# A light-weight convolution and a quick-GELU feed-forward: POOL sums and one tap's buffer change places

## The chip, the cores and the metric

One core of one Trainium2 chip runs the whole program. The metric is the time of one execution on the device in microseconds; less is better. Engines are named as in the profile: PE (TensorE: matmuls, PEld their weight loads), DVE (VectorE), ACT (ScalarE), POOL (GpSimd), SP (SyncE, which only issues DMAs). PSUM is the memory that PE writes; SBUF is the on-chip memory of all the others.

## What is computed

`x` has 8 batches of 4096 tokens of 192 channels. A causal convolution of 7 taps, whose weights are a softmax over the taps and are shared by 24 channels each, is followed by a feed-forward layer with 2048 hidden units. All is float32.

```python
def _attn_ref(x, weight):
    w = np.exp(weight - np.max(weight, axis=-1, keepdims=True))
    w = w / (np.sum(w, axis=-1, keepdims=True) + 1e-09)
    ...
    out = np.einsum('hk,bskhg->bshg', w, x_unf)      # x_unf: the last 7 tokens of each token
    return out.reshape(B, S, D)

def _moe_ref(x, w_in, w_out):                        # x: (32768, 192)
    h = x @ w_in
    g = h * (1.0 / (1.0 + np.exp(-1.702 * h)))
    return g @ w_out
```

## The kernel before

The 32768 tokens are worked on in 32 big steps. Each big step has two products. `hidden` (line 773) makes h and its GELU from the convolved x (the first product); `second` (line 1079) multiplies GELU(h) by w_out (the second product). Both use fast matrix multiplication: fewer matmuls than the plain product, in exchange for sums of operands before and of results after. Operands are summed in SBUF by DVE, by POOL and by accumulating DMAs; results are summed in PSUM and by DVE.

**The order is written by hand.** `HIDDEN` (line 738) and `PLAN` (line 1031) are lists of small actions; each engine gets its instructions in the order of these lists, and waits for others by semaphores. One execution of `hidden` runs `HIDDEN` once, one of `second` runs `PLAN` once. All of it is unrolled: `hidden(1), second(1), hidden(2), second(2), ...` An engine that waits holds back all that is queued behind on it.

- `("mm", v, t, to, first)` is one term of the first product: 4 matmuls of 512 columns into the PSUM tile `p<to>` (2 banks), there being 4 such tiles, p0 to p3. `HIDDEN` has 40 of them, and `("fetch",)` is a 41st: the first term of the next big step, left out in the last. The operand is a block of conv (`conv_t`, or for blocks 16 to 19 a place in `g`).
- `("copy", "a" or "v", dst, src, sign)` moves a PSUM tile by ACT or DVE, `join` adds two by DVE, `gelu` is ACT's GELU into `g`. The names k0 to k8 (`KS`, line 145) are SBUF tiles; k0 is `room[:, 1, :]`.
- `("main", form, spot, p, first)` and `("go", n)` in `PLAN` issue the second product's matmuls (line 1097); `side` adds a fourth chunk beside the three, whose result ACT copies out (line 1122). `sum` is a DVE sum of operands ("spots" of 128x1024 in SBUF), `acc` one by an accumulating DMA from POOL's queue (line 1073).

**Spots.** `spot(i)` (line 138) names a place of 128x1024 in SBUF: 0 and 1 lie in `osbs`, 2 to 4 in `room`, the others in `g`. `spot(2)` and k0 are the same memory. (s, 0) and (s, 2) below are the halves of spot s.

**The convolution** of big step n+2 is made during `second(n)` and the beginning of `hidden(n+1)`. `("tap",)` runs the next of 21 taps (line 559): ACT multiplies a shifted x by a tap's weight. They run over c = 1, 0, 2 (blocks of 64 channels; c = 1 is the middle one) and k = 0 to 6. Tap (c, 0) is written to the block itself, the others to a "home": the places listed in `TAP_SPOTS` and `TAP_HALVES` (lines 158 and 159), in order of k. For c = 2, POOL adds the homes one by one (line 565). For c = 1 and 0 a tree of accumulating DMAs from POOL's queue adds them (line 583): `LATER` (line 552) says behind which tap a stage (c, i, j) is issued, which adds home j to home i; i = 0 is the block itself. 17 of the taps run in `PLAN`, to tap (2, 2), and 4 in `HIDDEN`.

**The sums of conv** ("pieces"). Each term of the first product takes a block of conv or a sum of blocks. The raw blocks are 0 to 5 (c = 0: 0 and 1, c = 1: 2 and 3, c = 2: 4 and 5); blocks 6 to 15 are sums in one buffer in `conv_t`, so a block of the next big step may be written only when PE has read the old one for the last time. Blocks 16 to 19 lie in `g`, at spots 14 and 17 (`SPOT_V`). POOL makes them (`sum_of`, line 590; the instruction's line is 433 for a difference and 431 for a sum). Each block also has a crossed copy, its upper and lower 64 partitions exchanged, by two DMAs from SP's queue (`cross`, line 597). `over` in `HIDDEN` makes the two sums of block 12 and its crossing, `ve` blocks 13 and 14; the rest comes from `list_pieces` (line 649), which `("piece", n)` takes n at a time; `("late",)` runs all that is left ahead of the mark `None`, behind which the four sums of blocks 16 to 19 stand.

SP's queue also carries, in the order of the program, the output's stores (line 1025) and the loads of x (line 99).

Of the kernel before, what the change touches and what calls it, by code (L numbers as in the profile page):

```python
# [15 lines left out]
def kernel(  # L16
# [93 lines left out]
    sums = [psum.tile([P, TOK], F32, name=f"sums{h}") for h in range(2)]  # L110
# [5 lines left out]
    NG = 4  # L116
# [41 lines left out]
    TAP_SPOTS = {0: (10, 16, 15), 1: (1, 2, 11)}  # L158
    TAP_HALVES = {2: ((11, 2), (13, 0), (18, 0), (18, 2), (18, 0), (18, 2)), 3: ((12, 2), (16, 2), (15, 2), (16, 0), (15, 0), (12, 0))}
# [39 lines left out]
    def own(big):  # L199
        return conv_t[:, big % 2 * NR : big % 2 * NR + NR, :]  # L200

    SUMS_B = [
        (6, 1, "-", 5), (7, 2, "-", 4), (8, 12, "-", 2), (9, 2, "-", 3), (10, 0, "-", 12), (11, 14, "-", 8),
    ]
    SUMS_B_1 = [
# [4 lines left out]
    SUMS_E = [  # L210
        (13, 0, "-", 3), (14, 1, "-", 3),
    ]
    SUMS_S = [
        (15, 1, "-", 11),
    ]
    SUMS_L = [
        (16, 0, "-", 6), (17, 7, "-", 3), (18, 0, "-", 2), (19, 0, "-", 1),
# [321 lines left out]
    def conv(big, c, k, ns=slice(0, 2), times=vec.tensor_scalar_mul):  # L539
# [66 lines left out]
    def cross_spot(s):  # L606
        cross(spot(s)[:, 1:NG:2, :], spot(s)[:, 0:NG:2, :])
# [6 lines left out]
    LATE = sorted({s for s, k in SPOT_V.values()})  # L614

    def runs(b0, b1, n=3):
        return [(i, min(i + n, b1)) for i in range(b0, b1, n)]
# [16 lines left out]
    def make_late_1():  # L634
        for item in SUMS_L:
            sum_of(1, item, vec)
        for s in LATE:
            cross_spot(s)

    def make_rest_1():  # L640
        for item in SUMS_E + SUMS_S:
            sum_of(1, item, vec)
        for r in (V_S, V_E):
            if r[1] > r[0]:
                cross_run(1, *r, act.copy)
# [3 lines left out]
    def list_pieces(big):  # L649

        def add(f, *a):
            pieces.append(lambda: f(*a))

        for r in RAW_RUNS:
            add(cross_run, big, *r)
        if NV_E:
            add(cross_run, big, *V_E)
        for sums, block in ((SUMS_B, V_B), (SUMS_S, V_S)):
            for item in sums:
                add(sum_of, big, item)  # L660
            for r in runs(*block):
                add(cross_run, big, *r)
        pieces.append(None)
        for item in SUMS_L:
            add(sum_of, big, item)
        for s in LATE:
            add(cross_spot, s)
# [65 lines left out]
    def plain(u, m, n, v, slot, ks=range(NC), first=0):  # L733
# [39 lines left out]
    def hidden(big, tiles, work):  # L773
# [82 lines left out]
        def ve(i):  # L856
            if more:
                need(f"done {big + 1}")
                sum_of(big + 1, SUMS_E[i])

        do = dict(
            mm=mm, copy=copy, join=join, gelu=gelu, turn=turn, tap=tap, early=early, over=over, ve=ve,
# [154 lines left out]
    def store(big, n, o=None, queues=(nc.sync,) * 3):  # L1017
# [382 lines left out]
```

## Time and profile before

| | |
|---|---|
| runs of the kernel before | 2480.61 us median (2478.57, 2480.61, 2483.55) |
| the profiled execution, its own time | 2478.28 us |
| its span from the first to the last instruction | 2476.6 us |
| mean granted clock of TensorE | 0.968 |
| ACT busy, POOL busy | 1711.2 us (69%), 1093.7 us (44%) |
| DMA queues, share of 16 engines | POOL's (software) 44.7%, SP's (hardware) 27.2% |

A row such as `L710 PE MATMUL slot<-conv_t,w_in_s` reads: line 710 of the kernel, PE, a matmul into the tile `slot` from `conv_t` and `w_in_s`. Line 710 is the first product, line 1097 the second. In rows of waits, `A <- B: total, times, longest` says that A's engine sat idle and that B ended it. In a timeline, the columns are the start, the duration, then what ran, and in brackets the idle time before it and what ended that. In the table by windows, each row is a stretch of time: its length, then the busy time and (count) of PE, PEld, DVE, ACT and POOL, the granted clock of TensorE, the busy share of the DMA engines and GB/s.

### The profile page before, as it was taken

To read this page: it belongs to the slowest core of one execution; us is meant where nothing else is said; L and a number is where in the kernel's file an instruction comes from. 1 tells how busy PE (TensorE), PEld (TensorE's weight loads), DVE (VectorE), ACT (ScalarE), POOL (GpSimd) and SP (SyncE) were. 2 spreads that over 40 slices of the span, in tenths; PEclk is the share of its full clock that TensorE was granted. 3 is DMA by queue.
4 is the path that set the end of the run, shared out by engine and by line. 5 is a ranking of instruction groups with operands and counts; after the bars stand their busy time and mean duration, and the time that the engine had idled before them with its cause. 6 is when DMAs were issued, how large, how long until landed. Compare 5 with 4: busy or idle time off the path is not lost.

```text
span 2476.6 us, 63053 instructions
## 1 busy us (share of the span) xinstructions
PE 2336.8 (94%) x25090; PEld 1478.1 (60%) x25090; DVE 2129.1 (86%) x3059; ACT 1711.2 (69%) x3338; POOL 1093.7 (44%) x1218
## 2 busy tenths in 40 slices
PE   9899999999999999999999999999999999999999
PEld 4355656656665566556646565466666566764664
DVE  8998888898888988889888888888988888888898
ACT  8677676776666766767666677676776766767655
POOL 1553445434454444543445544455444554344520
PEclk9899999999999999999999999999999999999999
DMA  8976678866678666787667876678766788666753
GB/s 194 157 154 138 133 136 163 165 141 138 133 152 174 141 130 133 152 175 144 135 135 140 176 148 138 137 137 173 156 139 133 136 168 162 139 133 122 150 106 66
DMA packets 317127, 358.04 MB, mean 145 GB/s; under 512 B 123680, under 2 KB 226592, under 8 KB 316832
## 3 DMA queue, kind: packets, MB, share of 16 engines
q0 software_dynamic: 82192, 196.32, 44.7%
q1 hardware_dynamic: 232992, 157.29, 27.2%
q8 instruction: 199, 3.26, 0.5%
q14 instruction: 96, 0.79, 0.1%
q10 hardware_dynamic: 1648, 0.39, 0.1%
HBM read 53.15 MB, written 25.17 MB: 32 GB/s over the span
## 4 chain that ended last, share of the span: by engine, by line
PE 73%; DMA 13%; DVE 5%; issue 4%; POOL 3%; ACT 1%; SPq 0%; POOLq 0%; ACTq 0%; DVEq 0%
PE slot L710 34%; PE slot L1097 16%; PE sums L710 12%; PE sums L1097 11%; DMA g<-g 7%; DMA conv_t<-room 3%; DMA osbs<-osbs 3%; POOL g L433 1%; ACT room L800 1%; POOL conv_t L583 1%; POOL g L583 1%; DVE g L433 1%; DVE room L433 0%; DMA g<-in_moe_w_in_dram 0%; POOL g L1073 0%
## 5 line engine op out<-in xcount | busy, mean ns | idle before, releaser
L710 PE MATMUL slot<-conv_t,w_in_s 64*128 64x512 f32 x3372 | 935.4, 613 | 8.0 <-DVE osbs L1014 6.5
L1097 PE MATMUL slot<-g,w_form 128*32 128x256 f32 x5872 | 716.1, 379 | 6.5 <-DMA g<-g 5.7
L710 PEld LDWEIGHTS slot<-conv_t,w_in_s 64*128 64x128 f32 x3372 | 552.8, 196 | 252.0 <-issue 132.3
L433 DVE TENSOR_TENSOR g<-g 128x1024 f32<-128x1024 f32 x372 | 444.9, 1221 | 31.5 <-ACT g L826 28.2
L433 POOL TENSOR_TENSOR conv_t<-conv_t 128x256 f32<-128x256 f32 x300 | 283.8, 1018 | 399.5 <-PE slot L710 202.3
L1097 PE MATMUL sums<-g,w_form 128*32 128x256 f32 x3800 | 425.5, 379 | 6.8 <-DMA g<-g 6.6
L1097 PEld LDWEIGHTS slot<-g,w_form 128*32 128x32 f32 x5872 | 361.3, 110 | 100.9 <-DMA g<-g 12.0
L710 PE MATMUL sums<-conv_t,w_in_s 64*128 64x512 f32 x1284 | 408.4, 603 | 0.3 <-DVE w_in_s L416 0.3
L819 ACT ACTIVATE g<-slot 128x512 f32<-128x512 f32 x494 | 265.8, 624 | 129.4 <-PE slot L710 94.7
L565 POOL TENSOR_TENSOR conv_t<-conv_t,g 128x512 f32<-128x512 f32 x180 | 267.8, 1488 | 145.2 <-ACT g L563 140.3
L1097 PE MATMUL slot<-g,w_out_s 128*32 128x256 f32 x4080 | 321.3, 379 | 0.0
L1122 ACT COPY room<-slot 32x256 f32<-32x256 f32 x434 | 158.9, 366 | 220.9 <-PE slot L1097 214.4
L563 ACT ACTIVATE g<-xt,cw 128x512 f32<-128x512 f32 x418 | 287.7, 717 | 3.7
L710 PEld LDWEIGHTS sums<-conv_t,w_in_s 64*128 64x128 f32 x1284 | 209.0, 192 | 91.9 <-issue 43.5
L1097 PEld LDWEIGHTS sums<-g,w_form 128*32 128x32 f32 x3800 | 208.1, 110 | 80.8 <-DMA g<-g 13.5
L710 PE MATMUL slot<-g,w_in_s 64*128 64x512 f32 x556 | 201.0, 642 | 56.0 <-ACT room L800 48.1
L1097 PEld LDWEIGHTS slot<-g,w_out_s 128*32 128x32 f32 x4080 | 166.2, 110 | 125.8 <-ACT g L819 11.4
L1073 POOL DMA_DIRECT2D g<-g x124 | 126.9, 1023 | 231.6 <-DVE g L433 156.4
L800 ACT COPY room<-slot 128x512 f32<-128x512 f32 x246 | 137.4, 627 | 109.0 <-PE slot L710 48.8
L826 ACT ACTIVATE g<-g 128x1024 f32<-128x1024 f32 x155 | 170.4, 1100 | 0.4 <-DVE g L813 0.4
L1122 ACT COPY room<-sums 32x256 f32<-32x256 f32 x217 | 79.5, 366 | 115.5 <-PE sums L1097 110.6
L583 POOL DMA_DIRECT2D g<-g x145 | 147.3, 1016 | 26.1 <-ACT g L563 24.3
(246 smaller groups left out, 3973.5 us busy)
## 6 DMA issues: line engine op xcount, KB each, us to landing
g<-g POOLq DMA_DIRECT2D x124, 512.0 KB, 7.2
conv_t<-conv_t SPq DMA_DIRECT2D x240, 192.0 KB, 3.2
xin<-in_x_dram SPq DMA_DIRECT2D x240, 180.0 KB, 6.4
g<-g POOLq DMA_DIRECT2D x149, 256.0 KB, 6.6
out_dram<-osbs SPq DMA_DIRECT2D x186, 128.0 KB, 4.0
g<-g SPq DMA_DIRECT2D x124, 128.0 KB, 4.0
g<-room POOLq DMA_DIRECT2D x31, 512.0 KB, 6.6
conv_t<-g POOLq DMA_DIRECT2D x60, 256.0 KB, 4.7
```

Of the source, the lines that this page charges most:

```text
L433: eng.tensor_sub(v(dst), v(a), v(b))
L563: act.mul(home, conv_src(big, c, k), cw[:, c, k : k + 1])
L565: nc.gpsimd.tensor_add(dst, dst, home)
L583: nc.gpsimd.dma_start(out=out, in_=src, accum_op=ALU.add)
L710: nc.tensor.matmul(slot[h], w_in_s[halves[h], a, v * P : (v + 1) * P], src, start=first, stop=True, skip_group_check=True,)
L800: act.copy(out, i) if sign > 0 else act.mul(out, i, -1.0)
L819: act.activation(dst[:, :, h, :], ot(bank(src, h)), AF.Gelu_apprx_sigmoid, scale=float(sign))
L826: act.activation(dst.rearrange("p o h t -> p h o t"), src, AF.Gelu_apprx_sigmoid, scale=float(sign))
L1073: nc.gpsimd.dma_start(out=spot(dst), in_=spot(a), accum_op=ALU.add)
L1097: nc.tensor.matmul(dst, w, t, start=first, stop=last, skip_group_check=True)
L1122: act.copy(to, d)
```

## The change

Per big step the same 15 POOL sums are made, in another place. Blocks 8, 6 and 7 go from `PLAN` to `HIDDEN`, where blocks 13 and 14 already were; these five now stand at five places (`ve` 0 to 4). Block 15 stays in `PLAN`. Of the four sums at spots 14 and 17, block 19 goes from the end of `PLAN` to the following `HIDDEN` (`vl`), for the same big step. Each of these four is crossed behind its own sum, by two DMAs of 64x256, where two DMAs of 64x2x256 crossed a whole spot. The homes of the middle block (c = 1) for k = 1 to 6 were (1,0), (1,2), (2,0), (2,2), (11,0), (11,2); they become (1,0), (1,2), (11,0), (2,0), (2,2), (11,2). Five stages of the tap trees are issued behind later taps, and the pieces stand elsewhere in `PLAN`. The order of the instructions on PE, DVE and ACT is as before, but for the place that ACT's taps 3 to 5 of the middle block write.

```diff
-    TAP_SPOTS = {0: (10, 16, 15), 1: (1, 2, 11)}
+    TAP_SPOTS = {0: (10, 16, 15)}
...
+    TAP_HALVES = {1: ((1, 0), (1, 2), (11, 0), (2, 0), (2, 2), (11, 2)), 2: ...
...
-    SUMS_B = [
-        (6, 1, "-", 5), (7, 2, "-", 4), (8, 12, "-", 2), (9, 2, "-", 3), (10, 0, "-", 12), (11, 14, "-", 8),
-    ]
+    SUMS_H = [
+        (13, 0, "-", 3), (8, 12, "-", 2), (14, 1, "-", 3), (6, 1, "-", 5), (7, 2, "-", 4),
+    ]
+    SUMS_M = [
+        (9, 2, "-", 3), (10, 0, "-", 12), (11, 14, "-", 8), (15, 1, "-", 11),
+    ]
+    RUNS_H, RUNS_M = [(6, 9), (13, 15)], [(9, 12), (15, 16)]
...
-        (16, 0, "-", 6), (17, 7, "-", 3), (18, 0, "-", 2), (19, 0, "-", 1),
+        (16, 0, "-", 6), (17, 7, "-", 3), (18, 0, "-", 2),
+    ]
+    SUMS_LH = [
+        (19, 0, "-", 1),
     ]
...
     LATER = {
-        (1, 2): [(1, 1, 2)], (1, 4): [(1, 3, 4)], (1, 6): [(1, 5, 6), (1, 0, 1)], (0, 3): [(1, 3, 5)],
-        (0, 2): [(0, 1, 2)], (0, 4): [(0, 3, 4)], (0, 6): [(0, 5, 6), (0, 0, 1)], (2, 0): [(1, 0, 3)],
-        (2, 2): [(0, 3, 5)], (2, 5): [(0, 0, 3)],
+        (1, 2): [(1, 1, 2)], (1, 4): [(1, 3, 4)], (1, 6): [(1, 5, 6)], (0, 0): [(1, 0, 1)], (0, 2): [(0, 1, 2)],
+        (0, 4): [(0, 3, 4)], (0, 5): [(1, 3, 5)], (0, 6): [(0, 5, 6)], (2, 0): [(0, 0, 1)], (2, 2): [(1, 0, 3)],
+        (2, 3): [(0, 3, 5)], (2, 5): [(0, 0, 3)],
     }
...
-    def cross_spot(s):
-        cross(spot(s)[:, 1:NG:2, :], spot(s)[:, 0:NG:2, :])
+    def cross_spot(b):
+        both = pair(0, b)
+        cross(both[:, 1, :], both[:, 0, :])
...
         for r in RAW_RUNS:
             add(cross_run, big, *r)
-        if NV_E:
-            add(cross_run, big, *V_E)
-        for sums, block in ((SUMS_B, V_B), (SUMS_S, V_S)):
-            for item in sums:
-                add(sum_of, big, item)
-            for r in runs(*block):
-                add(cross_run, big, *r)
+        for r in RUNS_H:
+            add(cross_run, big, *r)
+        for item in SUMS_M:
+            add(sum_of, big, item)
+        for r in RUNS_M:
+            add(cross_run, big, *r)
         pieces.append(None)
         for item in SUMS_L:
             add(sum_of, big, item)
-        for s in LATE:
-            add(cross_spot, s)
+            add(cross_spot, item[0])
...
         def ve(i):
             if more:
                 need(f"done {big + 1}")
-                sum_of(big + 1, SUMS_E[i])
+                sum_of(big + 1, SUMS_H[i])
+
+        def vl(i):
+            if big > 1:
+                sum_of(big, SUMS_LH[i])
+                cross_spot(SUMS_LH[i][0])
```

`HIDDEN`, one action to a line, where it differs:

```diff
 ('mm', 0, 19, 3, 0)
 ('join', 'p1', 'p2', '+', 'k7')
+('vl', 0)
...
 ('over',)
+('ve', 0)
 ('mm', 0, 5, 1, 0)
...
 ('mm', 1, 17, 3, 0)
+('ve', 1)
...
 ('mm', 1, 1, 3, 1)
-('ve', 0)
-('ve', 1)
+('ve', 2)
...
 ('join', 'p1', 'k1', '-', 'k7')
+('ve', 3)
 ('copy', 'a', 'k4', 'p3', 1)
 ('mm', 1, 15, 2, 0)
+('ve', 4)
```

`PLAN` differs in its `piece` and `late` actions alone. Before, the pieces ahead of `late` (13: seven sums and six crossings) stood one by one, the first two together, behind the `go`s 2 to 27 of its 78, `late` behind the 30th, and the last six as 1, 1, 1, 1 and 2 behind the `go`s 60, 62, 64, 66 and 67. Now ten (four sums and six crossings) stand behind the `go`s 2 to 26, `late` behind the 27th, and the last six, three sums each with its crossing, as 2, 2 and 2 behind the `go`s 60, 62 and 64.

More of the change, by code (lines that the diff above doesn't have):

```diff
@@ L157 @@
     KEPT_LATE = 3
-    TAP_SPOTS = {0: (10, 16, 15), 1: (1, 2, 11)}
-    TAP_HALVES = {2: ((11, 2), (13, 0), (18, 0), (18, 2), (18, 0), (18, 2)), 3: ((12, 2), (16, 2), (15, 2), (16, 0), (15, 0), (12, 0))}
+    TAP_SPOTS = {0: (10, 16, 15)}
+    TAP_HALVES = {1: ((1, 0), (1, 2), (11, 0), (2, 0), (2, 2), (11, 2)), 2: ((11, 2), (13, 0), (18, 0), (18, 2), (18, 0), (18, 2)), 3: ((12, 2), (16, 2), (15, 2), (16, 0), (15, 0), (12, 0))}
     def kept(i):
@@ L209 @@
     SUMS_F = [(12, 1, "+", 4), (12, 12, "-", 5)]
-    SUMS_E = [
-        (13, 0, "-", 3), (14, 1, "-", 3),
-    ]
-    SUMS_S = [
-        (15, 1, "-", 11),
+    SUMS_ES = [
+        (13, 0, "-", 3), (14, 1, "-", 3), (15, 1, "-", 11),
     ]
     SUMS_L = [
-        (16, 0, "-", 6), (17, 7, "-", 3), (18, 0, "-", 2), (19, 0, "-", 1),
+        (16, 0, "-", 6), (17, 7, "-", 3), (18, 0, "-", 2),
+    ]
+    SUMS_LH = [
+        (19, 0, "-", 1),
     ]
@@ L613 @@
     FIRST = V_F if NV_F else (FB, FB + 1)
-    LATE = sorted({s for s, k in SPOT_V.values()})
     def runs(b0, b1, n=3):
@@ L634, in make_late_1 @@
     def make_late_1():
-        for item in SUMS_L:
+        for item in SUMS_L + SUMS_LH:
             sum_of(1, item, vec)
-        for s in LATE:
-            cross_spot(s)
+        for b in SPOT_V:
+            cross_spot(b)
     def make_rest_1():
-        for item in SUMS_E + SUMS_S:
+        for item in SUMS_ES:
             sum_of(1, item, vec)
@@ L665, in list_pieces @@
             add(sum_of, big, item)
-        for s in LATE:
-            add(cross_spot, s)
+            add(cross_spot, item[0])
     def next_piece(n=1):
@@ L744 @@
         ("mm", 0, 18, 0, 0), ("tap",), ("mm", 0, 17, 2, 1), ("join", "k8", "p1", "-", "k2"),
[19 rows of a table removed]
[17 rows of a table added]
+        ("early", 5), ("gelu", 14, "p1", 1), ("mm", 1, 18, 0, 0), ("gelu", 12, "p2", 1), ("early", 2),
+        ("gelu", 15, "p0", 1), ("gelu", 13, "o13", 1),
     ]
@@ L858, in ve @@
                 need(f"done {big + 1}")
-                sum_of(big + 1, SUMS_E[i])
+                sum_of(big + 1, SUMS_H[i])
[3 more added lines that the diff above has]
+                cross_spot(SUMS_LH[i][0])
         do = dict(
-            mm=mm, copy=copy, join=join, gelu=gelu, turn=turn, tap=tap, early=early, over=over, ve=ve,
+            mm=mm, copy=copy, join=join, gelu=gelu, turn=turn, tap=tap, early=early, over=over, ve=ve, vl=vl,
             fetch=lambda: fetch(big + 1, tiles[NEXT[0]]) if more else None,
@@ L1031 @@
     PLAN = [
[36 rows of a table removed]
[7 rows of a table added]
+        ("sum", 0, 0, "+", 5), ("main", 14, 2, "p2", 0), ("go", 2), ("acc", 15, 4), ("piece", 1), ("tap",),
[7 rows of a table added]
+        ("sum", 13, 18, "+", 4), ("tap",), ("go", 2), ("sum", 6, 9, "-", 5), ("tap",), ("go", 1), ("acc", 12, 9),
[19 rows of a table added]
     ]
```

105 rows, old and new, of tables (HIDDEN, PLAN) are left out of this document.

## The prediction

> **What bounds the kernel now.** I read the page's engine rows first, then PE's waits.
>
> ```profile
> span 2476.6 us, 63053 instructions
> ...
> PE 2336.8 (94%) x25090; PEld 1478.1 (60%) x25090; DVE 2129.1 (86%) x3059; ACT 1711.2 (69%) x3338; POOL 1093.7 (44%) x1218
> ```
>
> ```profile
> PE sums L710 <- ACT room L800: 54.8, 15, 4.3
> PE slot L710 <- ACT room L800: 48.1, 13, 4.6
> ...
> PE sums L1097 <- DMA g<-g: 6.6, 11, 1.3
> PE slot L1097 <- DMA g<-g: 5.7, 8, 1.4
> ```
>
> PE is the engine with the least idle time, and nearly all of it has one releaser: 28 waits of 102.9 us together, 3.7 us each, for an ACT copy into `room`. They come once per big step, at the beginning of the first product. The waits of the second product sum to 12.3 us. What one wait costs in all is seen when the first products, `hidden(2)` to `hidden(30)`, are cut out as 29 windows, the second products behind them as 29 more, and the last big step beside them.
>
> ```profile
> 1177.40:1220.40 43.00, 39.25 (x168) 30.90 (x164) 35.33 (x50) 29.19 (x54) 18.31 (x21) 0.92 0.53 107
> 1254.90:1296.40 41.50, 37.86 (x168) 18.20 (x164) 33.12 (x50) 29.30 (x54) 18.06 (x20) 0.96 0.55 111
> ...
> sum 1223.10, PE 1113.82 PEld 773.58 DVE 1002.05 ACT 847.36 POOL 526.06; mean PE 38.41 PEld 26.68 DVE 34.55 ACT 29.22 POOL 18.14
> ```
>
> ```profile
> 1910.30:1944.60 34.30, 33.98 (x625) 20.07 (x624) 30.97 (x43) 24.12 (x51) 17.41 (x22) 1.00 1.00 196
> ...
> sum 999.10, PE 986.22 PEld 582.28 DVE 900.39 ACT 689.34 POOL 493.80; mean PE 34.01 PEld 20.08 DVE 31.05 ACT 23.77 POOL 17.03
> ```
>
> ```profile
> 2402.10:2437.30 35.20, 35.20 (x168) 16.74 (x164) 30.17 (x47) 26.67 (x50) 0.87 (x1) 1.00 0.19 38
> 2437.30:2471.20 33.90, 33.85 (x625) 20.15 (x624) 29.67 (x43) 12.94 (x34) 4.28 (x5) 1.00 0.45 85
> ```
>
> ```profile
> 1206.41 0.86 PE sums L710 x4
> ```
>
> The mean first product is 1223.10 / 29 = 42.18 us. The last one, with no taps around it and no wait, takes 35.20 us for 40 terms; with the 41st (4 matmuls, 0.86 us by the chain's row) 36.06. So each of the 29 loses 6.12 us, 177 us in all: 3.7 us as the wait and some 2.4 us since the clock granted behind it is halved for a while (0.92 or 0.96 over the window, 1.00 in the last). The second product has 34.45 us against 33.90, 16 us in all. These 193 us are all there is to win.
>
> Who is late at that place? The chain of waits over one boundary, PE's, ACT's and POOL's timelines there:
>
> ```profile
> 1254.22 0.68 POOL g L433
> 1254.90 5.67 DMA conv_t<-room
> ```
>
> ```profile
> 1254.87 1.13 PE L710 MATMUL slot<-conv_t,w_in_s 64*128 64x512 f32 x4
> ...
> 1261.36 1.66 PE L710 MATMUL slot<-g,w_in_s 64*128 64x512 f32 x3 [3.64 <-ACT room L800]
> ```
>
> ```profile
> 1255.42 1.34 ACT L563 ACTIVATE g<-xt,cw 128x512 f32<-128x512 f32 x2
> 1260.67 1.07 ACT L800 COPY room<-slot 128x512 f32<-128x512 f32 x2 [3.91 <-DMA conv_t<-room]
> ```
>
> ```profile
> 1247.09 0.86 POOL L583 DMA_DIRECT2D room<-g  x1 [3.18 <-DVE sums L431]
> ...
> 1251.70 0.73 POOL L433 TENSOR_TENSOR g<-conv_t 128x256 f32<-128x256 f32 x1 [2.85 <-DVE osbs L1014]
> ...
> 1253.53 2.05 POOL L433 TENSOR_TENSOR g<-conv_t 128x256 f32<-128x256 f32 x2
> 1254.90 1.50 POOL L583 DMA_DIRECT2D conv_t<-room  x1
> ```
>
> `conv_t<-room` is stage (1, 0, 3), behind tap (2, 0): the middle block takes up the home of its third tap, (2,0), which is `room[:, 1, :]`, which is k0. The ACT copy is k0 from p1, the first evacuation of the first product. It may not overwrite k0 before that stage has read it, at 1260.57, and the term of block 16, the fourth, needs p1. On POOL the stage stands behind the sums of blocks 16 to 18.
>
> **The change, part by part.**
>
> *The third tap's place, and the stages.* Spot 2 now holds taps 4 and 5. Its readers are the stages (1, 3, 4), early, and (1, 3, 5), behind tap (0, 5); stage (1, 0, 3) reads spot 11, which `hidden` writes only in its middle (GELUs 5 and 7). Stage (1, 3, 5) is today's `room<-g`, at 1247.09; behind tap (0, 5) and one more DMA of the kind (0.86 us) it would be issued at about 1248.
>
> ```profile
> room<-g POOLq DMA_DIRECT2D x29, 256.0 KB, 6.4
> ...
> conv_t<-conv_t SPq DMA_DIRECT2D x122, 64.0 KB, 3.1
> ```
>
> ```profile
> g<-g SPq DMA_DIRECT2D x124, 128.0 KB, 4.0
> ```
>
> With 6.4 us it lands at 1254.4, before PE begins the first product and more than 2 us before ACT could write k0. The wait goes: gain 6.12 us a step. Five stages spread over later taps add no DMA; (0, 0, 3) still stands behind tap (2, 5), and the sums behind it have till the 41st term. I cost them at nothing; were block 12 late, the wait would stand at that term, 31 us in.
>
> *A new wait.* The third tap now writes spot 11, which DVE reads in `sum 20, 20, -, 11`, the last of three, and PE in the two `go`s just before the tap.
>
> ```profile
> 1232.32 3.61 DVE L433 TENSOR_TENSOR g<-g 128x1024 f32<-128x1024 f32 x3
> ```
>
> ```profile
> 1235.19 0.72 ACT L563 ACTIVATE room<-xt,cw 128x512 f32<-128x512 f32 x1
> ```
>
> The tap ran at 1235.19, the DVE sums end at 1235.93: ACT is 0.74 us later. Queued behind on ACT are the seed of p1 for a term six `go`s on and the copies of PE's side chunks; six `go`s are 2.6 us (33.90 / 78 each), so PE need not wait. I cost it at nothing, 0.74 a step if that cover were gone.
>
> *What is late next* decides what is left of the 6.12 us.
>
> (a) ACT's two taps end at 1256.76, 1.89 us after PE's start at 1254.87; copying k0 takes 1.07, so p1's halves are free at about 2.4 and 3.0. PE wants them behind three terms, at 2.57: 0 to 0.5 us, I take 0.3.
>
> (b) The fifth term needs p0, which DVE empties into k5 behind the last joins and transposes of the second product.
>
> ```profile
> 1177.45 1.13 PE L710 MATMUL sums<-conv_t,w_in_s 64*128 64x512 f32 x4
> ```
>
> ```profile
> 1178.39 2.95 DVE L431 TENSOR_TENSOR room<-room 96x256 f32<-96x256 f32 x1
> ...
> 1181.74 1.25 DVE L802 COPY g<-slot 128x512 f32<-128x512 f32 x2
> ...
> 2403.07 0.38 DVE L431 TENSOR_TENSOR room<-room 96x256 f32<-96x256 f32 x1
> ```
>
> ```profile
> 1179.18 3.28 POOL L565 TENSOR_TENSOR conv_t<-conv_t,g 128x512 f32<-128x512 f32 x2
> ```
>
> That join of 0.38 us takes 2.95 beside POOL's adds, and the copy ends at 1182.99, 5.54 us after PE's start; without the delay of 2.57 it would be 2.97. PE wants the tile behind four terms, at 3.43. So 0 to 2.1 us. One POOL sum (block 19) no longer stands ahead of the adds, so the join should find its gap sooner, after the first add: I take 0.5.
>
> (c) The crossed half of block 16. Before, four SP DMAs stood behind two sums.
>
> ```profile
> 1254.92 4.34 SPq L597 DMA_DIRECT2D g<-g  x4
> ```
>
> One issue is 1.1 us. Now the first pair stands behind its own sum, which ends at 1252.43: issued by 1253.5, landed 3.1 (the 64 KB row) to 4.0 (the 128 KB row) later, at 1256.6 to 1257.5, or 1.7 to 2.6 us after PE's start, against 2.57: 0 to 0.1 us, I take 0.1.
>
> *The sums.* POOL makes the same 15 per step. Three leave the second product for the first, where POOL idles:
>
> ```profile
> POOL conv_t L433 <- PE slot L710: 202.3, 31, 10.0
> POOL conv_t L433 <- PE sums L710: 194.8, 30, 10.0
> ...
> POOL g L1073 <- ACT g L819: 103.7, 27, 4.5
> ```
>
> Each waits for PE's last read of its block; the last, block 7, stands behind the 30th term. Queued behind it is the DMA `acc 8, 0`, which waits for ACT's GELUs behind the 39th term anyway. Cost nothing; if a sum came late, that DMA would carry it into the second product. There, POOL no longer blocks SP's crossings: 0 to 0.55 us a step, I take 0.15, as the DMA engines' share of 1.00 leaves little. The crossed halves are read in the next first product only.
>
> *SP.* Four more DMAs a step, of half the size, 4 x 1.1 us of issue on a queue that nobody waits for at that time: the stores go 2 us later, block 19's pair stands behind them and has till the 35th term. Nothing.
>
> Beside this stands a rule of the Trainium skill, "SBUF — State Buffer", section "Who interferes with whom": a DVE instruction with two SBUF inputs and a POOL instruction that reads SBUF exclude each other, the later one waiting for the whole of the other. The join of 2.95 us agrees. The rule speaks against the sums' new place, since DVE's early operand sums in `HIDDEN` have two SBUF inputs; by it the sum would be the first rival's.
>
> **The sum.** Left over: 0.3 + 0.5 + 0.1 = 0.9 us. Gain: 29 x (6.12 - 0.9) = 151, and 29 x 0.15 = 4 in the second product, together 155. The profiled execution's own time is 2478.28 (span 2476.6 and 1.7 around it); 2478.3 - 155 = 2323. It is 2.3 under the median of the runs, so I predict 2325 for the median.
>
> **The rivals.**
>
> 1. *DVE becomes the bound of the first product.* It is busy 34.55 of 42.18 us there; in 36 us little room is left. If the six sums that now stand in it (13, 8, 14, 6, 7, 19) each stop DVE for a POOL sum of 0.73 us, it is 34.55 + 4.4 = 38.9 us, and the gain 3.2 x 29 = 94: 2386. For it: the row of 2.95 us. Against it: 2.2 us of DVE's 34.55 are that delayed join and can go, and DVE's joins mostly read PSUM.
>
> 2. *The wait moves to block 16.* If its crossing lands as late as today's first pair, 1254.92 + 1.1 + 4.0 = 1260.0, 5.1 us after PE's start, PE waits 2.6 us, the clock is halved for 1.7, and with the 0.9 of above 5.2 us stay: gain 27 us, 2453. For it: the DMA share. Against it: issue 2.4 us earlier, half the bytes.
>
> 3. *The change doesn't free k0.* If stage (1, 3, 5) lands where `conv_t<-room` did, at 1260.57, all stays: 2480. For it: it still reads k0's memory. Against it: 7 us between the two issues.
>
> 4. *Slower: the accumulation `acc 18, 14` lands later.* PE waits for it near the end of the second product.
>
> ```profile
> 1241.44 1.41 POOL L1073 DMA_DIRECT2D g<-g  x1
> ```
>
> ```profile
> 1251.27 0.42 PE L1097 MATMUL sums<-g,w_form 128*32 128x256 f32 x3 [0.44 <-DMA g<-g]
> ```
>
> Issued at 1241.44, it lands just before 1251.27, 9.8 us later, in a stage with a DMA share of 1.00. Eight crossings now come together at that product's start. Each us later is a us per step; from 5.2 on it eats the gain, and if its 9.8 us became 15.8 the time would be 2325 + 29 x 6 = 2499. Against it: no bytes are added, and the crossings come earlier than this DMA, not beside it.
>
> **How the numbers follow.** Forecast 0.60, rival 1 0.18, rival 2 0.09, rival 3 0.07, rival 4 0.06. With nothing left over and the second product at 33.90 the time is 2480.6 - 193 = 2287; that is the low end. The high end, 2400, is rival 1 with some more. A difference within 0.2% (5 us) can't be told from none. Faster: 0.60 + 0.18 + 0.09 + 0.02 of rival 3 = 0.89; same: 0.04 of rival 3; slower: 0.06 + 0.01 = 0.07.
>
> **What would show it.** Right: PE's waits for ACT `room` fall from 102.9 to under 20 us; the windows of the first product average 36.5 to 37.5 us at a clock of 1.00; the ACT copy into k0 follows its two taps at once. Rival 1: no wait at the start, but PE waiting for DVE within the first product. Rival 2: PE waiting for a DMA `g<-g` at the fourth term. Rival 3: PE's rows as before, with `g<-room` as ACT's releaser. Rival 4: longer waits of L1097 for `g<-g`, and a second product over 35 us. I am wrong at the root if the clock stays at 0.92 to 0.96 in the first product though k0 is free.

## The result, and the profile after

The changed kernel takes 2450.03 us (median of 4 runs, 2448.70 to 2455.13), the kernel before 2480.12 beside it. The ratio is 0.9881, with a 95% interval of 0.9863 to 0.9898: 1.2% faster, 30 us where 155 were forecast, and outside the range that was given. The profiled execution took 2455.13 us.

The engine rows of the page, then DVE's, ACT's and PE's waits in the changed kernel:

```profile
span 2453.4 us, 63569 instructions
...
PE 2345.3 (96%) x25090; PEld 1451.0 (59%) x25090; DVE 2120.7 (86%) x3059; ACT 1712.5 (70%) x3338; POOL 1082.9 (44%) x1218
```

```profile
DVE osbs L815 <- DMA out_dram<-osbs: 105.3, 24, 5.6
...
ACT g L567 <- DVE g L437: 43.6, 29, 2.1
...
PE slot L712 <- DVE sums L815: 34.3, 15, 3.6
...
PE sums L712 <- DVE slot L815: 26.7, 14, 3.6
...
DVE osbs L815 <- PE slot L712: 20.8, 5, 4.6
...
PE sums L1103 <- DMA g<-g: 14.0, 14, 2.0
...
PE slot L1103 <- DMA g<-g: 9.8, 14, 2.1
```

The 102.9 us for ACT's copy into `room` are gone. In their place PE waits 61.0 us for DVE's joins in the first product, 29 times. DVE itself waits 105.3 us, 24 times, for something that no row of before names: an output store. Five more waits of the same join, 20.8 us, are put down to PE; but in all 29 steps the join starts 0.12 us behind the landing of the last store, so all 126 us belong to the stores.

The 29 windows of the first product (`hidden(2)` to `hidden(30)`; one of them and the sum), then the sum of the second products:

```profile
1236.90:1277.10 40.20, 38.28 (x168) 20.45 (x164) 34.00 (x50) 29.08 (x54) 18.01 (x19) 0.96 0.57 115
...
sum 1163.70, PE 1099.03 PEld 707.82 DVE 973.74 ACT 847.32 POOL 517.48; mean PE 37.90 PEld 24.41 DVE 33.58 ACT 29.22 POOL 17.84
```

```profile
sum 1032.80, PE 1008.51 PEld 614.05 DVE 920.08 ACT 690.55 POOL 491.60; mean PE 34.78 PEld 21.17 DVE 31.73 ACT 23.81 POOL 16.95
```

The first product falls from 42.18 to 40.13 us (59.4 us over 29 steps, forecast 151), the second rises from 34.45 to 35.61 (33.7 us, where 4 were to be won). Together that is -25.7; the profiled executions differ by 23.2.

One boundary of the changed kernel, as the timelines of PE, ACT, DVE and SP have it:

```profile
1236.91 1.13 PE L712 MATMUL slot<-conv_t,w_in_s 64*128 64x512 f32 x4
...
1246.89 1.91 PE L712 MATMUL slot<-conv_t,w_in_s 64*128 64x512 f32 x7
1250.71 1.81 PE L712 MATMUL sums<-conv_t,w_in_s 64*128 64x512 f32 x3 [1.92 <-DVE slot L815]
```

```profile
1237.47 1.34 ACT L567 ACTIVATE g<-xt,cw 128x512 f32<-128x512 f32 x2
1238.83 1.07 ACT L802 COPY room<-slot 128x512 f32<-128x512 f32 x2
```

```profile
1237.86 1.02 DVE L435 TENSOR_TENSOR room<-room 96x256 f32<-96x256 f32 x1
...
1243.57 1.27 DVE L815 TENSOR_TENSOR g<-room,slot 128x512 f32<-128x512 f32 x2
1248.76 1.29 DVE L815 TENSOR_TENSOR osbs<-slot,room 128x512 f32<-128x512 f32 x2 [3.92 <-DMA out_dram<-osbs]
```

```profile
1239.84 6.06 SPq L1032 DMA_DIRECT2D out_dram<-osbs  x6
```

The boundary itself is as forecast: ACT's two taps, then at once the copy of k0 at 1238.83, and PE goes on. At 1244.84, eight microseconds in, DVE comes to `join k8 = p1 - k2`. k8 is `KS[8]`, the second half of `osbs`, and `osbs` is also where the outputs are staged: the six stores that SP issues between 1239.84 and 1245.90 read it, the last three the half that k8 takes. The join may not overwrite what a store hasn't read. DVE stands for 3.92 us, and the joins that free PE's next tiles stand behind it; PE runs out of a free tile at 1248.8 and waits 1.92.

The same two places in the kernel before:

```profile
1259.36 5.79 SPq L1025 DMA_DIRECT2D out_dram<-osbs  x6
```

```profile
1268.30 1.28 DVE L813 TENSOR_TENSOR osbs<-slot,room 128x512 f32<-128x512 f32 x2
```

By the landing records of the 29 steps, the last store landed 12.08 us after PE's start before and 12.27 after. The stores got hardly later; the join got earlier. Before, PE's wait for k0 carried it to 13.43 us after PE's start (1268.30 - 1254.87), 1.2 us behind the last landing of that step (0.35 to 3.34 us over the 29 steps, 1.86 in the mean), and no wait was to be seen.

### The profile page after: what moved, and what is told of

Its sections match the earlier page's. It is cut to its first block, busy times and chain, and to the rows that moved or that the text cites. A ratio compares the mean times of both kernels' runs of the same rounds, so it can differ in the third digit from the quotient of the medians.

```text
span 2453.4 us, 63569 instructions
## 1 busy us (share of the span) xinstructions
PE 2345.3 (96%) x25090; PEld 1451.0 (59%) x25090; DVE 2120.7 (86%) x3059; ACT 1712.5 (70%) x3338; POOL 1082.9 (44%) x1218
## 4 chain that ended last, share of the span: by engine, by line
PE 32%; DVE 29%; DMA 19%; ACT 7%; issue 7%; POOL 3%; SPq 2%; DVEq 0%; POOLq 0%; ACTq 0%
PE slot L712 16%; DMA g<-g 11%; DVE g L437 9%; PE sums L712 7%; PE slot L1103 6%; DMA out_dram<-osbs 5%; DVE room L437 4%; PE sums L1103 3%; DVE slot L815 2%; DVE osbs L435 2%; ACT room L802 2%; DVE g L815 2%; DVE osbs L437 2%; DVE sums L815 2%; SPq L1032 2%
## 5 line engine op out<-in xcount | busy, mean ns | idle before, releaser
L712 PE MATMUL slot<-conv_t,w_in_s 64*128 64x512 f32 x3372 | 958.1, 601 | 44.9 <-DVE sums L815 34.3
L1103 PE MATMUL slot<-g,w_form 128*32 128x256 f32 x5872 | 730.7, 381 | 9.9 <-DMA g<-g 9.8
L712 PEld LDWEIGHTS slot<-conv_t,w_in_s 64*128 64x128 f32 x3372 | 515.7, 190 | 310.5 <-issue 102.6
L712 PE MATMUL sums<-conv_t,w_in_s 64*128 64x512 f32 x1284 | 445.5, 613 | 27.0 <-DVE slot L815 26.7
L1103 PE MATMUL sums<-g,w_form 128*32 128x256 f32 x3800 | 435.2, 381 | 14.0 <-DMA g<-g 14.0
L437 POOL TENSOR_TENSOR conv_t<-conv_t 128x256 f32<-128x256 f32 x300 | 262.6, 945 | 315.1 <-issue 155.3
L1079 POOL DMA_DIRECT2D g<-g x124 | 134.6, 1085 | 428.8 <-PE slot L1103 200.7
L567 ACT ACTIVATE g<-xt,cw 128x512 f32<-128x512 f32 x418 | 289.4, 724 | 47.8 <-DVE g L437 43.6
L569 POOL TENSOR_TENSOR conv_t<-conv_t,g 128x512 f32<-128x512 f32 x180 | 282.1, 1567 | 17.3 <-ACT g L567 14.6
L712 PE MATMUL slot<-g,w_in_s 64*128 64x512 f32 x556 | 214.0, 625 | 0.5 <-POOL conv_t L569 0.5
L1103 PE MATMUL slot<-osbs,w_form 128*32 128x256 f32 x1240 | 146.9, 380 | 0.5 <-ACT slot L1132 0.3
```

What stands on the lines that cost most here:

```text
L437: eng.tensor_sub(v(dst), v(a), v(b))
L567: act.mul(home, conv_src(big, c, k), cw[:, c, k : k + 1])
L569: nc.gpsimd.tensor_add(dst, dst, home)
L712: nc.tensor.matmul(slot[h], w_in_s[halves[h], a, v * P : (v + 1) * P], src, start=first, stop=True, skip_group_check=True,)
L1079: nc.gpsimd.dma_start(out=spot(dst), in_=spot(a), accum_op=ALU.add)
L1103: nc.tensor.matmul(dst, w, t, start=first, stop=last, skip_group_check=True)
```

## The experiments

Two renamings are used again and again, so they are shown once. *k off the store*: k8 takes the home of k4, which is free from the 8th term to the 29th; k4's second life takes that of k2 (free from the 18th), and k7's first life that of k3 (free from the 7th to the 16th). Nothing is computed in another way.

```diff
-("join", "k8", "p1", "-", "k2"), ("copy", "a", "k7", "p0", 1)
+("join", "k4", "p1", "-", "k2"), ("copy", "a", "k3", "p0", 1)
-("join", "p1", "p2", "+", "k7") ... ("join", "o6", "p0", "-", "k8")
+("join", "p1", "p2", "+", "k3") ... ("join", "o6", "p0", "-", "k4")
-("copy", "a", "k4", "p3", 1) ... ("join", "p3", "k8", "-", "k3") ... ("join", "p2", "p0", "+", "k4")
+("copy", "a", "k2", "p3", 1) ... ("join", "p3", "k4", "-", "k3") ... ("join", "p2", "p0", "+", "k2")
-("join", "o13", "k4", "+", "p0")
+("join", "o13", "k2", "+", "p0")
```

*Tap root*: the middle block's third and fourth taps in spot 2, fifth and sixth in spot 11, and the tree of stages ends in the fifth's home.

```diff
-1: ((1, 0), (1, 2), (11, 0), (2, 0), (2, 2), (11, 2))
+1: ((1, 0), (1, 2), (2, 0), (2, 2), (11, 0), (11, 2))
-(0, 5): [(1, 3, 5)] ... (2, 2): [(1, 0, 3)]
+(0, 5): [(1, 5, 3)] ... (2, 2): [(1, 0, 5)]
```

### Is it the store?

> Changed kernel in which k8 and the first life of k7 no longer lie in the output staging: k8 takes the home of k4 (free from the 8th to the 29th term), k4's second life that of k2, k7's first life that of k3. Theory: what is left of the loss in the first product (40.1 us a step against 36.1) is DVE's wait for the output stores, 4.4 us of DVE and some 2.1 us of PE a step, and the half clock behind it. Then the first product falls to about 36.4 us, 29 x 3.7 = 107 us: about 2343 us (2330 to 2365), no wait of DVE for out_dram<-osbs, no wait of PE for DVE's joins at 12 to 15 us. Rival 1: DVE is late by its own work and only stood idle in a place where it would be late anyway: about 2410 to 2450. Rival 2: another landing comes at the same place (a crossed half or a tap stage): 2390 to 2440, with a new releaser named in PE's waits.

The change with *k off the store*. Measured: 2328.41 us, ratio 0.9384 (0.9369 to 0.9398), just under the theory's range. DVE no longer waits for `out_dram<-osbs`; the windows of the first product sum to this:

```profile
sum 1041.20, PE 1040.18 PEld 595.35 DVE 986.67 ACT 838.21 POOL 531.28; mean PE 35.87 PEld 20.53 DVE 34.02 ACT 28.90 POOL 18.32
```

35.90 us a step, with PE busy 35.87 of them. The whole rest of the first product's loss hung on this one wait, more than the theory said (36.4). What it cost a step is now read off: 40.13 - 35.90 = 4.23 us. 2.20 of them are PE's idle time (40.13 - 37.90 there, 0.03 left here) and 2.03 are matmuls that ran longer (37.90 - 35.87): in the changed kernel 14 of the 29 windows have a granted clock of 0.92 or 0.96, here all 29 have 1.00. DVE is busy 34.02 of 35.90 us, and in these 29 products PE doesn't wait for it once: rival 1 had no hold.

> The kernel before with the same renaming of k8, k7 and k4. Theory: the stores' landing was hidden behind the ACT copy of k0 (the join came 1.2 us behind the last landing in the step looked at), so the wait for room stays at 3.7 us a step and the time hardly moves: 2465 to 2482 us. Rival: the stores already cost time before, beside the copy of k0: 2430 us or less.

The kernel before with the same edit. Measured: 2478.94 us, ratio 0.9991 (0.9982 to 1.0001), with PE's wait for k0 still there (110.0 us):

```profile
PE sums L710 <- ACT room L800: 57.4, 15, 4.8
...
PE slot L710 <- ACT room L800: 52.6, 14, 4.4
```

The same edit is worth 122 us in the changed kernel and nothing that can be measured in the one before. The two waits stand one behind the other: as long as the first is there, the second costs nothing.

> Changed kernel with k8 alone in the home of k4 (and k4's second life in that of k2); k7 stays in the first half of the output staging, whose stores land at 8.8 us in the mean. Theory: DVE's wait for the last store is what counts, ACT's for the third (17 us in all) costs PE little: 2328 to 2345 us. Rival: the copy of k7 now waits in the open, as PE needs its two halves for the next product: 2345 to 2390.

The edit is the first one without its two lines on k7. Measured: 2340.25 us, as the theory says. ACT's copy of k7 into the first half waits 17.0 us in all for its store; without that wait too it is 12 us less, in the first run.

### Why do the stores land so late?

> Changed kernel without the three tap stages behind the taps (2, 0), (2, 2) and (2, 3), DMAs of 256 KB each that are issued on POOL from 1 us before to 5 us into the first product; their additions are left out of the convolution. SP's queue is as it was. Theory: the stores land late because the DMA engines are full (a share of 1.04, 0.86, 1.02 and 0.77 in the four stretches of 3 us from the start of the first product): without 0.75 MB of 180 GB/s, 4 us of their time, the last store lands some 3 us sooner, at about 9 us; DVE's wait for it falls from 4.4 to 1 or 2 us, and PE's wait behind it nearly goes: 2340 to 2380 us. Rival: the order on SP makes them late, the stores standing behind the crossings of blocks 17 and 18: the landing stays at 11 us or later, the time at 2430 to 2450.

```diff
-for b, i, j in LATER.get((c, k), ()) if big > 2 else ():
+for b, i, j in LATER.get((c, k), ()) if big > 2 and (c, k) not in ((2, 0), (2, 2), (2, 3)) else ():
```

Measured: 2333.34 us, a little under the theory's range. The first 12 us of a first product in stretches of 3 us, of the changed kernel and then of this one, with SP's timeline:

```profile
1236.90:1239.90 3.00, 3.00 (x17) 1.37 (x14) 2.80 (x6) 2.77 (x6) 2.92 (x3) 1.00 1.04 193
1239.90:1242.90 3.00, 3.00 (x15) 1.73 (x15) 2.46 (x5) 3.00 (x8) 3.00 (x5) 1.00 0.86 176
1242.90:1245.90 3.00, 3.00 (x16) 1.57 (x14) 1.95 (x4) 2.54 (x5) 2.65 (x3) 1.00 1.02 187
1245.90:1248.90 3.00, 2.90 (x13) 1.31 (x9) 0.14 (x1) 1.26 (x4) 0.54 (x1) 1.00 0.77 140
```

```profile
1186.40:1189.40 3.00, 3.00 (x17) 1.37 (x14) 2.81 (x5) 2.78 (x6) 2.84 (x3) 1.00 0.75 164
1189.40:1192.40 3.00, 3.00 (x15) 2.21 (x15) 2.72 (x5) 3.00 (x7) 1.79 (x2) 1.00 0.90 192
1192.40:1195.40 3.00, 3.00 (x17) 2.49 (x15) 3.00 (x6) 2.99 (x6) 1.29 (x2) 1.00 0.38 81
1195.40:1198.40 3.00, 3.00 (x17) 2.50 (x15) 2.77 (x6) 0.75 (x2) 2.77 (x3) 1.00 0.51 87
```

```profile
1188.58 3.57 SPq L1032 DMA_DIRECT2D out_dram<-osbs  x6
```

SP's queue is untouched, its six stores are issued in 3.57 us in place of 6.06, and the last lands 7.86 us after PE's start in place of 12.27 (means of 29). DVE's wait for the stores falls to 1.4 us in all. So the order on SP does not make the stores late; these three transfers do, by the load that they put on the DMA engines: the share over the 12 us is 0.92 in the mean with them and 0.64 without. The Trainium skill, "DMA: Bandwidth & Descriptors", section "Issuing engines are not separate DMA queues", says that transfers started by different engines run on the same 16 DMA engines and interleave there; the 4.4 us that SP's stores gain when three transfers of POOL's go agree with it.

### The parts of the change, one by one

> Kernel before with the third tap's place and the spread stages alone: no sum is moved, the crossing of blocks 16 to 19 stays in four DMAs of whole pairs. Theory: the wait for k0 goes, and DVE's wait for the stores comes up in its place, since the stores land just as late (some 12 us into the first product) with the old crossing too: 2435 to 2465 us, DVE idle for out_dram<-osbs about 100 us. Rival: the split crossing, eight DMAs of 64 KB on SP in place of four of 128 KB ahead of the stores, is what made the stores late: without it they land 2 us sooner, DVE waits half as long, and the time is 2370 to 2400.

```diff
-TAP_SPOTS = {0: (10, 16, 15), 1: (1, 2, 11)}
+TAP_SPOTS = {0: (10, 16, 15)}
+TAP_HALVES = {1: ((1, 0), (1, 2), (11, 0), (2, 0), (2, 2), (11, 2)),
...
```

With it goes `LATER` as the change has it.

Measured: 2421.93 us, ratio 0.9768 (0.9736 to 0.9800): neither. The tap's place alone is 28 us faster than the whole change. Its waits:

```profile
DVE osbs L813 <- DMA out_dram<-osbs: 53.7, 23, 4.3
...
ACT g L563 <- DVE g L433: 22.7, 28, 2.0
...
PE slot L710 <- DMA g<-g: 21.4, 10, 2.8
...
PE sums L710 <- DMA g<-g: 15.3, 8, 2.6
...
PE slot L710 <- DVE sums L813: 14.2, 11, 2.0
...
PE sums L710 <- DVE slot L813: 10.6, 9, 2.2
```

The last store lands at 12.73 us here, so the old crossing doesn't make it sooner, and the rival falls. PE now waits 36.7 us for the crossed half of block 16, at the fourth term, and 24.8 for the joins behind the store. Six more waits at the fourth term, 11.5 us, are put down to ACT; but in these six too the term starts 0.13 to 0.14 us behind the landing of that half, so the crossing costs 48 us. The changed kernel has 61.0 for the joins alone. Moving the sums and splitting the crossing took away a wait that stood ahead of the same landing, and the first product gained nothing by it: it takes 1161.6 / 29 = 40.06 us here and 40.13 there. The difference is in the second product: 1007.4 / 29 = 34.74 against 35.61.

> Kernel before with the third tap's place, the stages, and k8, k7 and k4 renamed as in the first run: with that run it shows what the move of the sums and the split crossing are worth when nothing covers them. Theory (as predicted: 0.15 us a step for the sums, and a little for DVE's late join behind block 19's sum): 2328 to 2345 us. Rival: the sums' move matters once the first product is free of waits, since block 16's crossing stands behind two sums and lands late, or DVE's join is held by POOL's adds: 1 to 2 us a step, 2357 to 2390.

The kernel of the run above with k off the store. Measured: 2386.03 us, ratio 0.9606 (0.9562 to 0.9649). The rival holds: with the store out of the way, the old crossing costs PE 45.2 us (53 with four waits at the same place that are put down to ACT),

```profile
PE sums L710 <- DMA g<-g: 24.3, 12, 3.0
...
PE slot L710 <- DMA g<-g: 20.9, 10, 2.8
```

and the first product takes 38.72 us (1122.9 / 29) where the split crossing has 35.90. So the moved sums and the split crossing are worth 58 us (2386 against 2328) once nothing stands behind them, and cost 28 as long as the store does. Which of the two frees block 16, its place ahead of the other sums or the smaller DMAs, no run separates.

> Changed kernel with the third tap's place and the stages of before: only the sums are moved and the crossing is split. Theory: the wait for k0 is back at about 3.7 us a step, and the sums are worth nothing: 2470 to 2485 us. Rival: with block 19's sum gone from ahead of it, the stage behind tap (2, 0) is issued up to 1 us sooner, and some of the wait goes: 2445 to 2465.

The diff of the tap's place alone, the other way round, on the changed kernel. Measured: 2457.75 us, ratio 0.9915 (0.9890 to 0.9939), the rival's range. The moved sums and the split crossing are worth some 21 us by themselves (2478.32 beside it). The wait for k0, and the sum of the second products:

```profile
PE sums L712 <- ACT room L802: 46.6, 13, 4.1
...
PE slot L712 <- ACT room L802: 43.4, 12, 4.1
```

```profile
sum 997.60, PE 988.13 PEld 581.82 DVE 922.55 ACT 693.52 POOL 485.46; mean PE 34.07 PEld 20.06 DVE 31.81 ACT 23.91 POOL 16.74
```

The rival's time came, its mechanism hardly: the stage is issued 0.17 us sooner, not 1. The 90.0 us look shorter than the 102.9 of before, but five more waits at this place are put down to others (two before): 106.7 us in all against 110.7. Most of what the first product gains (41.61 us against 42.18) is PE's busy time, 37.98 us against 38.41, with a window clock of 0.92 in 8 steps in place of 12. The second product takes 997.6 / 29 = 34.40 us: with the tap in its old place the moved sums cost it nothing.

### Why did the second product grow?

> Changed kernel in which the middle block's third and fourth taps go to spot 2 and the fifth and sixth to spot 11, with the sum of the tree ending in the fifth tap's home instead of the third's, so that the last stage still reads spot 11. Theory: ACT's wait of 1.5 us a step for the DVE sum on spot 11 goes; with it the 0.4 us that PE loses at the 43rd go, and the late issue of the tap stages ahead of acc 18, 14, which costs 0.5 us a step at the 70th go. The second product falls from 35.6 to about 34.7 us: 2424 us (2415 to 2435); the stores' wait stays. Rival: acc 18, 14 lands late by the load of the DMA engines and not by the taps: only 0.4 us a step, 2438 us.

The change with *tap root*. Measured: 2416.82 us, ratio 0.9750 (0.9728 to 0.9773), as the theory says. ACT waits for no DVE sum any more, and the second product falls to 1002.0 / 29 = 34.55 us:

```profile
sum 1002.00, PE 989.65 PEld 581.91 DVE 921.64 ACT 690.37 POOL 493.14; mean PE 34.13 PEld 20.07 DVE 31.78 ACT 23.81 POOL 17.00
```

```profile
PEld slot L1103 <- DVE room L437: 17.1, 29, 0.6
...
PE sums L1103 <- DMA g<-g: 7.5, 6, 3.0
...
PE slot L1103 <- DMA g<-g: 2.8, 1, 2.8
```

So the late tap made 1.06 us of the 1.16. It cost PE little at its own place: at the 50th `go` PE is 0.30 us behind the kernel before (mean start of that matmul over the steps), where it was 0.38. The rest comes later, since the stages wait for the taps and `acc 18, 14` is queued behind the stages: PE's waits for `g<-g` fall from 23.8 us to 10.3. The 0.30 belong to a DVE join that is late without the tap too, 29 times, the first row. They are made good at the 71st `go`, where the kernel before waits for `acc 18, 14`: there PE is 0.07 us behind.

> Changed kernel in which the third of the sums that POOL makes in a row near the beginning of the second product (block 11) comes one place later, behind acc 15, 4; nothing else is moved but the crossings behind it. Theory: three POOL sums in a row hold one DVE sum for 3.66 us in place of 1.2, which makes DVE's sum on spot 11 and with it ACT's tap late: 1.5 us a step, against 0.8 where the tap's place alone was changed. With two in a row the tap waits some 0.8 us, the second product falls from 35.6 to about 34.9 us: 2430 us (2422 to 2440). Rival: the third sum holds another DVE sum instead, and the time does not change: 2445 to 2455.

```diff
-("go", 1), ("piece", 1), ("go", 1),
-("sum", 0, 0, "+", 5), ("main", 14, 2, "p2", 0), ("go", 2), ("acc", 15, 4), ("piece", 1), ("tap",),
+("go", 2),
+("sum", 0, 0, "+", 5), ("main", 14, 2, "p2", 0), ("go", 2), ("acc", 15, 4), ("piece", 1), ("tap",),
```

The edit moves block 15's sum one place on as well. Measured: 2448.85 us, ratio 0.9895 (0.9870 to 0.9919), the rival's range; the change has 0.9881. What suggested it was this, DVE's and POOL's timelines near the beginning of a second product of the changed kernel:

```profile
1357.01 4.91 DVE L437 TENSOR_TENSOR g<-g 128x1024 f32<-128x1024 f32 x2
```

```profile
1358.40 2.43 POOL L437 TENSOR_TENSOR conv_t<-conv_t 128x256 f32<-128x256 f32 x3
```

Two sums of 1.2 us each take 4.91, that is 2.5 longer, about the 2.43 of POOL's three. In the mean of the 29 steps DVE's sum there, `sum 4, 5, -, 10`, takes 3.28 us in the changed kernel and 1.80 before, and the sum on spot 11 ends 16.34 us after the product's start, where it was 15.55. So the tap waits 1.5 us in place of 0.81. With the tap's old place the sum ends just as late, at 16.36, and no tap waits for it. With the third sum moved away `sum 4, 5, -, 10` still takes 2.82 us, and another DVE sum, `sum 8, 6, -, 13`, takes 1.73 in place of 1.27: the sum on spot 11 ends at 16.15, and the tap's wait only falls from 43.6 to 39.6 us. So the rival holds: the moved sum holds DVE at another place.

### Both edits, and all three

> Both edits of the two runs on the changed kernel together. Theory: they lie in different products and add: 2343 - 26 = 2317 us (2300 to 2340), close to what was predicted for the change. Rival: with the first product shorter, the DMA engines, busy all through the second product, become what sets its end, and the sum is not reached: 2340 or more, with longer waits for g<-g in the second product.

Measured: 2300.54 us, ratio 0.9271 (0.9258 to 0.9285). They nearly add: 121.6 and 33.2 us by themselves, 149.5 under the change together, with 35.93 us for the first product and 34.43 for the second (1042.0 and 998.4 over 29). This beats both kernels.

> Changed kernel with k8, k7 and k4 renamed, the tap root in spot 11's later half, and the third sum of the run one place later. Theory: of the 0.3 us a step that PE still loses near the 43rd go without the tap's wait, most goes: 2290 to 2297 us. Rival: nothing is left there that this sum sets: 2297 to 2304 as without it.

Measured: 2305.39 us, ratio 0.9307 (0.9290 to 0.9325), no better than without the moved sum. Neither range held. The second product takes 1008.1 / 29 = 34.76 us; why it is slower stays open.

## Why the prediction missed

**The third tap's place: right.** The wait for k0 is gone, and of the 6.12 us a step that were to come back, 42.18 - 35.90 = 6.28 do come back with *k off the store*. In the change itself 2.05 come. One part of the working was too kind: stage (1, 3, 5) was to land before PE's start, and lands 0.40 us behind it in the mean; ACT's copy comes at 1.91 in every step, so that cover was enough.

**The step that failed** is the one on SP: "a queue that nobody waits for at that time: the stores go 2 us later ... Nothing". Somebody does wait: k8 and k7 lie in the store's source, and the join that writes k8 stood 1.2 us behind the last landing, for no other reason than the wait that was to be removed. The list under *What is late next*, (a) to (c), is short by this item, and it is the largest: 4.23 us a step, 123 us. That the stores would go 2 us later was wrong as well (12.08 us to 12.27), and didn't matter.

**How the miss adds up.** 155 us were forecast, and the windows give 25.7. The stores take 123 of the difference and the second product 38 (33.7 lost, 4 to be won); 31 come back, since the first product needs nothing of what was set aside for (a) to (c). That the run with *k off the store* takes 2328 us, beside the forecast of 2325, is luck: its first product gains 182 us where 151 were forecast, and its second loses 28 (1027.1 against 999.1) where 4 were to be won.

**(a) to (c): too dear.** 0.9 us a step was set aside for them; without the store wait nothing is left over, 35.90 us against the 36.06 of the last step and a 41st term. DVE's join of 2.95 us takes 1.02 at the boundary shown. The reason given for (c) holds: with the old crossing PE does wait at that place.

**The new wait on spot 11: wrong in cover.** Priced at 0.74 us of ACT, it is 0.81 with the tap alone (22.7 / 28), and nearly twice that, 1.5, in the whole change (43.6 / 29). "PE need not wait" holds at its own place, within 0.1 us; what "I cost it at nothing" left out is that the tap stages wait for these taps and are POOL DMAs ahead of `acc 18, 14`. "Five stages spread over later taps ... at nothing" is the same mistake seen from POOL.

**The sums: priced by themselves, dear together with the tap.** 0.15 us a step was to be won in the second product. With the tap's old place 0.05 is (34.45 to 34.40). The tap's place alone costs 0.29 (34.74), and both together 1.16 (35.61). The moved sums make DVE's sum on spot 11 0.8 us late, which costs nothing until a tap waits for it, and the prediction costed the two parts of the change one by one. The Trainium skill, "SBUF — State Buffer", section "Who interferes with whom", has a rule that bears on it, a DVE instruction with two SBUF inputs and a POOL instruction that reads SBUF shutting each other out. The 4.91 us agree. The prediction weighed that rule in the first product, where sums were added and where it cost PE nothing, and not in the second, where they were only put in another order.

**The rivals.** Rival 2 gave 2453, close to what came, by a mechanism that was not at work in the change: a coincidence. The runs with the old crossing show that the danger was real, with 48 us of waits at the fourth term. Rival 4's signs came true, with a second product of 35.61 us and 23.8 us of waits for `g<-g` in place of 12.3, but as the smaller of two terms, and by the tap stages and not by the crossings. Rival 1's sign, PE waiting for DVE within the first product, came true to the letter, and the rival falls all the same: DVE was late because it stood idle for a store. Without that wait it is busy 95% of the first product, and PE does not wait for it.

## What to carry to other kernels

A wait that is removed lets everything behind it run earlier, by its whole size: for each instruction in that stretch, list what else it depends on and how long ago that was done, down to the DMAs that still read what it writes. A dependency with less slack than the wait is long is the next wait, and the profile of before, where it never waited, has no row for it. Buffers that double as output staging are the place to look first.

## What the runs showed of the hardware

A store of 128 KB took 2.5 us from issue to landing in the median without the three stages of 256 KB, and 4.5 with them; SP's time to issue six of them went from 3.57 to 6.06 us along with it, so load on the DMA engines is also seen in the issuing queue.

The clock follows PE's pauses unevenly: behind the 1.92 us of the boundary shown the granted clock is halved for 3.4 us (0.96 over that window), and behind 2.46 us in this earlier one it is not (1.00):

```profile
333.60:373.00 39.40, 36.94 (x169) 22.47 (x165) 33.37 (x50) 29.23 (x54) 17.74 (x19) 1.00 0.58 115
```

```profile
348.17 1.29 PE L712 MATMUL sums<-conv_t,w_in_s 64*128 64x512 f32 x3 [2.46 <-DVE slot L815]
```
